# Where the low part of the first weight piece is computed, and a new order for the opening of a fused attention and feed-forward kernel

## The chip, the cores and the metric

The kernel runs on one core of one Trainium2 chip. The metric is the device time of one execution in microseconds (us). TensorE is called PE in the rows, its weight loads PEld, VectorE DVE, ScalarE ACT, GpSimd POOL, SyncE SP; a "q" behind a name is that engine's instruction queue, DMA issues included.

## The reference

A linear attention with a decaying state runs over 768 steps for 4 x 8 heads of 48 channels, and its output goes through a feed-forward layer without biases:

```python
for t in range(S):                                   # B=4, H=8, S=768, D=48
    cur = np.einsum('bhd,bhe->bhde', u[None] * kt, vt)
    y[:, :, t] = np.einsum('bhd,bhde->bhe', rt, state + cur)
    state = wt[:, :, :, None] * state + np.einsum('bhd,bhe->bhde', kt, vt)
x = y.transpose(0, 2, 1, 3).reshape(B * S, H * D)    # 3072 x 384
h = x @ w_in                                         # 384 x 2048
g = h * (1.0 / (1.0 + np.exp(-1.702 * h)))
out = g @ w_out                                      # 2048 x 384
```

All inputs and the output are float32.

## The kernel before

**Tiling.** The 3072 tokens are 24 chunks of 128 tokens, in 6 groups of 4 chunks. Attention works by chunk: VectorE scans the decays (L421, L427) and scales keys and queries (L442, L443), PE forms their products (L450, L476, L507, L525), ScalarE builds diagonal masks (L496), VectorE masks the scores (L576), and PE sums the output of the chunk into `ps_y` (L570, L615, L619). The feed-forward layer works by task: a task is one group (512 tokens) and one block of 128 of the 2048 hidden channels. Its first product (L679) is followed by the gelu (L690 or L694 on ScalarE, L695 on VectorE) and the second product (L709 to L711, later in the row-tiled form of L735).

**Split operands.** A float32 operand is held as two fp32r tiles, a rounded high part and the low part that is left, and each product is made of three: high by high, high by low, low by high. The output of a chunk is split by L633 (ScalarE writes the high part), L637 (PE adds minus the identity times the high part to the same PSUM bank) and L638 (ScalarE copies what is left there). Chunk 3, the last of the first group, is the last that is split before the first task can run, and `fill_x` (L647, token x2) then has twelve issues on SP and POOL move parts of x of chunks 0 to 2 to other partitions; the first task's first three matmuls read the three blocks of x that are so filled.

**Weights.** They arrive in 1 MB pieces (`raw`). `convert(i)`, the tokens "w i", unpacks one: ScalarE L224 and L225, VectorE L227 and L230, ScalarE L233 writes the high part into `pair`, VectorE L235 subtracts it and so writes the low part. Piece 0 is the first that a task needs, pieces 2 and 1 follow.

**Order.** Instructions are issued on each engine in the order of emission. For the opening (the first 20 tasks of 96, and chunks 0 to 10) that order is the hand-written string `RAMP`, whose tokens `do` carries out one by one (L859): "l 4" is a load of chunk 4, "a 3" the next step of chunk 3, "g 0", "h 0" and "y 0" are first product, gelu and second product of task 0, and "k 3" stands for three filler matmuls (`keep_clock`, L724) on a constant tile, whose result nothing uses. A planner orders what comes after `RAMP`. `ps_h` is a pool of two PSUM buffers (tag "ph") that the first products take in turn.

Of the kernel before, what the change touches and what calls it, by code (L numbers as in the profile page):

```python
# [8 lines left out]
F32 = mybir.dt.float32  # L9
# [5 lines left out]
ALU = mybir.AluOpType  # L15
# [6 lines left out]
P = 128  # L22
# [11 lines left out]
NL = SL // 2  # L34
# [26 lines left out]

FIRST = 20
RAMP = """
l0 M l0 a0 a0 a0 l0 k13 a0 a0 l1 l1 l2 a0 a0 a1 k4 a0 a1 f2 a1 l1 a0 l3 a0 k1 a1 a1 a1 a1 a2 f2 k3 a0 a0 w2 a1 a1 a2
f0 a2 k1 a0 a1 a1 l2 a2 a2 a2 k3 a1 a2 l3 a3 f0 a1 a2 a2 a2 w0 a3 f1 a3 a1 k2 a3 a2 f4 a3 w0 a3 k3 a2 a3 a3 a3 l4 a2
w0 a3 a3 a2 a4 f6 w0 a3 w2 x2 a3 w1 w1 k5 a3 k3 g0 f6 w2 g1 l4 w2 a4 h0 g2 f4 a4 w1 w1 h1 g3 w4 h2 w4 f3 a4 a4 a4 f8
y0 w3 f5 l5 g4 w3 h3 m4 l6 w4 a4 y1 w4 a4 w3 a4 g5 a5 w3 y2 a4 h4 a5 l5 a5 h5 y3 g6 w5 w5 m5 y4 a4 a5 w6 w6 h6 f7 w5
w5 w6 a5 w6 a6 g7 f8 w8 a5 y5 l6 w8 h7 g8 g9 w7 y6 a6 a6 a4 w7 a5 y7 w8 w8 a6 f10 h8 f9 u a5 a6 h9 w7 a6 a5 g10 w9
l7 f10 g11 a5 w7 a6 w9 l8 m6 a5 l7 a7 h10 y8 y9 w9 a6 w10 a7 g12 f11 w9 a6 y10 a7 h11 h12 a5 l9 w11 a7 w10 w11 a7 m7
a7 w10 a7 w11 y11 w10 y12 w11 a6 a7 g13 a7 a8 l8 h13 l9 g14 a6 a8 a8 g15 l10 a8 y13 h14 a7 m8 a7 a8 a8 h15 a9 a9 y14  # L70
a8 x7 y15 a8 a9 l10 a8 g16 g17 h16 m9 a9 h17 a9 a9 l11 g18 a9 y16 a10 a8 h18 y17 a9 g19 a10 a10 a8 a10 a9 a10 h19
m10 a10 l11
"""
WIDE = 512
CROSS = 6
HALF = 6
GAP = 3
ALONE = (HALF, 8)
THIRDS = [(m, (2 * m + i) * TOP // D, (2 * m + i) * TOP % D, i == 0) for m in range(NM) for i in range(2)]
WP = NF * DM // NL  # L80
SPLIT = range(FIRST, len(TASKS) - 1)
# [7 lines left out]
def rwkv_ffn_kernel(ctx: ExitStack, tc, wkr, vp, vrk, ub, w_in, w_out, masks, vt, uc, out):  # L89
    nc = tc.nc  # L90
    V, A, G, T = nc.vector, nc.scalar, nc.gpsimd, nc.tensor
# [5 lines left out]
    ps_h = ctx.enter_context(tc.tile_pool(name="ps_h", bufs=2, space=PSUM))  # L97
# [16 lines left out]
    ident = cp.tile([P, P], F32, name="ident")  # L114
# [12 lines left out]
    minus = wt.tile([P, P], F32R, tag=f"w{2 * NL - 2}", name="minus")  # L127
# [88 lines left out]
    def convert(i, pool, clamp):  # L216

        st = staged.pop(i)
        c = pool.tile([P, WP], I32, tag="c", name="c", bufs=2)
        w = st.rearrange("p k (n two) -> p (k n) two", two=2)  # L220
        l, h = w[:, :, 0], w[:, :, 1]
        cf = c.bitcast(F32)
        sums = {} if clamp else dict(accum_out=acc_sum[:, i : i + 1])
        A.activation(l, l.bitcast(U32), AF.Copy, scale=L_SCALE)  # L224
        A.activation(cf, h.bitcast(F32), AF.Abs, scale=W_SHIFT, **sums)  # L225
        yield
        V.scalar_tensor_tensor(h, h, -(2 ** 31), l, op0=ALU.bitwise_and, op1=ALU.bitwise_or)  # L227
        if clamp:
            V.tensor_scalar(cf, cf, W_MAX, None, op0=ALU.min)
        V.scalar_tensor_tensor(c, c, 3, h, op0=ALU.logical_shift_left, op1=ALU.bitwise_or)  # L230
        yield
        pair = pairs[i] = wt.tile([P, 2, WP], F32R, tag=f"w{i}", name=f"pair{i}")
        A.copy(pair[:, 0], cf)  # L233
        yield
        V.tensor_tensor(pair[:, 1], cf, pair[:, 0].bitcast(F32), op=ALU.subtract)  # L235
        yield

    def weight(which, f, m):

# [47 lines left out]
    def one_run(here, ahead):  # L287

        def emit(lists, before=None):

            mm = None
            for x in lists:
                if x:
                    out, w, moving, start, stop = x.pop(0)
                    mm = T.matmul(out, w, moving, start=start, stop=stop, skip_group_check=True)  # L295
                    if before:
                        tc.add_manual_dep(mm.ins, before, SYNC, reason="the other row tile is done with these rows")
                        before = None
            return mm

        same, other = ([ahead[r_][r_ ^ n] for r_ in range(2)] if ahead else [[], []] for n in range(2))
        before = None
        for beside in (other, same) if here else ():
            rows = here.pop(0)
            while max(map(len, rows)):
                mm = emit(rows, before)
                emit(beside)
                before = None
            if beside is other:
                for _ in range(GAP):  # L310
                    emit(same)
                nop = T.nop()
                tc.add_manual_dep(nop.ins, mm.ins.name, SYNC, reason="the rows of the bank change row tiles")
                before = nop.ins.name
        while max(map(len, same + other)):
            emit(same + other)

    def token_halves(t, kf, qf, kt, v, s, sf):
# [17 lines left out]
        for p in range(NP):  # L336
            for h in range(2):
                for b in range(2):
                    ahead[h][b].append(
                        (scores[h][half[b], p], kf[head(h), p, half[b]], qf[head(h), p, half[b]], True, True)  # L340
                    )
        if t in ALONE:
            one_run([], ahead)
# [64 lines left out]
    def chunk(t):  # L408
# [128 lines left out]
        def straight(ps, pair, low, high, rhs):  # L537

            for m in range(NM):
                for h in range(2):  # L540
                    yield ps[h * HB : (h + 1) * HB, m], pair(m, h), rhs(m, h)
            for m, h, d0, up in THIRDS:
                out_, w_ = (ps[P - 2 * TOP :, m], high) if up else (ps[0:TOP, m], low)
# [287 lines left out]
    def count(oks):  # L831

        ps = ps_a.tile([1, 1], F32, tag="psa", name="ps_n")
        T.matmul(ps, oks, oks, start=True, stop=True)
        V.tensor_copy(cnt, ps)
# [5 lines left out]
    with tc.manual_schedule():  # L841
# [7 lines left out]
        running, told = {}, {}  # L849

        def piece(kind, i):

            if (kind, i) not in running:
                running[kind, i] = {
                    "l": load, "e": decays, "a": chunk, "m": measures.get, "w": lambda i: convert(i, su, False), "r": rows_of, "f": fetch
                }[kind](i)
            next(running[kind, i])

        def do(token):  # L859
            kind, i = token[0], int(token[1:] or 0)  # L860
            told[token] = told.get(token, 0) + 1
            if kind in "lamwrfe":
                piece(kind, i)
                if kind == "w" and all(told.get(f"w{n}") == 4 for n in range(2 * NL)):
                    early.close()
                    pools["late"] = fast.enter_context(tc.tile_pool(name="late", bufs=2))
            elif kind == "x":
                group, col = where[i]
                if col == CHUNKS[group] - 1 - (group == 0):
                    fill_x(xs[group], 0, (col + 1) * C)  # L870
            elif kind == "u":
                nc.sync.dma_start(u_sb, ub)
                for x, fill, compare in ((eye, 0.0, ALU.not_equal), (later, 1.0, ALU.is_gt)):
                    G.memset(x, fill)
                    for h in range(2):
                        G.affine_select(
                            out=x[h * HB : (h + 1) * HB], in_=x[h * HB : (h + 1) * HB], pattern=[[1, HB]], base=0,
                            channel_multiplier=-1, compare_op=compare, fill=1.0 - fill,
                        )
            elif kind == "M":  # L880
                A.dma_start(hm[TOP:R2], masks)
                G.dma_start(um[TOP:R2, 0 : H // 2], masks[:, 2 : 2 + H // 2])
                for h in range(2):
                    rows, others = (slice(g * D, (g + 1) * D) for g in (h, 1 - h))
                    G.dma_start(um[TOP:R2][rows, H // 2 :], masks[others, 2 + H // 2 :])
                for x in states + [v[:, 0:TOP] for v in values] + padded:
                    G.memset(x, 0.0)
                A.activation(minus, ident, AF.Copy, scale=-1.0)
            elif kind == "k":
                for _ in range(i):  # L890
                    keep_clock()
            elif kind == "g":
                if i == len(TASKS) - 1:
                    count(counted.pop())
                first_product(i, TASKS[i])
            elif kind == "h":
                gelu(i, TASKS[i])
            elif kind == "y":
                second_product(i, TASKS[i])
            if kind == "y" or kind == "r" and told[token] == 2:  # L900
                i -= LAG if kind == "r" else 0
                parts.pop(i, None)
                group = TASKS[i][0]
                if i == last[group]:
                    if group == len(CHUNKS) - 1:
                        counted.append(nc.values_load(cnt, min_val=0, max_val=full))
                    store(group, starts[group] * C, CHUNKS[group] * C, (1, 0, 2) if kind == "r" else range(NM))
# [44 lines left out]
        for token in RAMP.split():  # L952
            do(token)
# [11 lines left out]
    n = counted[0]  # L965
# [104 lines left out]
```

## Time and profile before

| | us |
|---|---|
| median of 3 runs (lowest, highest) | 485.99 (485.84, 487.25) |
| the profiled execution | 485.96 |
| its span, first to last instruction | 484.2 |
| PE busy in the span | 475.0 (98%) |
| VectorE busy in the span | 289.6 (60%) |
| ScalarE busy in the span | 256.7 (53%) |

The profiled execution lies 0.03 us under the median, and 1.76 us of it lie outside the span. The shares of the whole span hide that it has stages: VectorE's 60% are an average over an opening in which it hardly rests and a later part in which it has little to do.

### The profile page before, as it was taken

To read this page: it belongs to the slowest core of one execution; us is meant where nothing else is said; L and a number is where in the kernel's file an instruction comes from. 1 tells how busy PE (TensorE), PEld (TensorE's weight loads), DVE (VectorE), ACT (ScalarE), POOL (GpSimd) and SP (SyncE) were. 2 spreads that over 40 slices of the span, in tenths; PEclk is the share of its full clock that TensorE was granted. 3 is DMA by queue.
4 is the path that set the end of the run, shared out by engine and by line. 5 is a ranking of instruction groups with operands and counts; after the bars stand their busy time and mean duration, and the time that the engine had idled before them with its cause. 6 is when DMAs were issued, how large, how long until landed. Compare 5 with 4: busy or idle time off the path is not lost.

```text
span 484.2 us, 14345 instructions
## 1 busy us (share of the span) xinstructions
PE 475.0 (98%) x5915; PEld 406.1 (84%) x5915; DVE 289.6 (60%) x455; ACT 256.7 (53%) x611; POOL 106.6 (22%) x222
## 2 busy tenths in 40 slices
PE   7999999999999999999999999999999999999995
PEld 4768888888888888888888888888888888888884
DVE  8999999998776456546656566666574221112120
ACT  5988898875653534634545545545645422422222
POOL 4051000002132406434407235406200002100000
PEclk9999999999999999999999999999999999999998
DMA  8868955235532305224305134205120001100002
GB/s 313 289 251 322 306 166 151 50 100 128 157 86 80 100 3 132 92 74 115 95 8 149 69 101 115 81 20 132 46 89 2 3 1 34 66 2 1 1 0 72
DMA packets 20728, 48.47 MB, mean 100 GB/s; under 512 B 4816, under 2 KB 10032, under 8 KB 20656
## 3 DMA queue, kind: packets, MB, share of 16 engines
q1 hardware_dynamic: 12128, 26.72, 16.6%
q0 software_dynamic: 8128, 20.24, 15.0%
q8 instruction: 48, 0.79, 0.7%
q10 hardware_dynamic: 400, 0.53, 0.3%
q14 instruction: 24, 0.20, 0.1%
HBM read 40.49 MB, written 4.72 MB: 93 GB/s over the span
## 4 chain that ended last, share of the span: by engine, by line
PE 95%; DVE 1%; DMA 1%; issue 1%; ACT 0%; SPq 0%; ACTq 0%; PEldq 0%; DVEq 0%
PE po L735 32%; PE ph L735 30%; PE ph L679 9%; PE ps_c L295 5%; PE ps_a L295 3%; PE po L709 3%; PE po L711 3%; PE po L710 3%; PE ps_d L450 1%; PE ps_y L619 1%; PE ps_t L476 1%; PE ps_y L532 1%; PE ps_s L525 1%; PE ps_t L470 1%; PE idle L724 1%; DMA wkr_t<-in_wkr 1%
## 5 line engine op out<-in xcount | busy, mean ns | idle before, releaser
L735 PE MATMUL ph<-x,pair 64*128 64x512 f32 x1350 | 220.6, 377 | 0.0
L735 PE MATMUL po<-gh,pair 64*128 64x512 f32 x912 | 185.9, 383 | 0.2 <-SPq L740 0.2
L735 PEld LDWEIGHTS ph<-x,pair 64*128 64x128 f32 x1350 | 170.2, 186 | 17.8 <-ACT gf L694 0.6
L695 DVE TENSOR_TENSOR gl<-gf,gh 128x512 fp32r<-128x512 f32 x96 | 66.1, 690 | 146.7 <-ACT gf L694 146.7
L694 ACT ACTIVATE gh<-ph 128x512 fp32r<-128x512 f32 x84 | 49.9, 594 | 150.7 <-PE ph L735 143.5
L735 PEld LDWEIGHTS po<-gh,pair 64*128 64x128 f32 x912 | 113.7, 186 | 12.4 <-issue 0.6
L735 PE MATMUL po<-gl,pair 64*128 64x512 f32 x456 | 117.1, 376 | 0.0
L735 PEld LDWEIGHTS po<-gl,pair 64*128 64x128 f32 x456 | 58.8, 186 | 5.7
L647 POOL DMA_DIRECT2D x<-x x33 | 16.6, 511 | 169.2 <-DVE x L248 127.1
L694 ACT ACTIVATE gf<-ph 128x512 f32<-128x512 f32 x84 | 49.6, 590 | 0.0
L679 PE MATMUL ph<-x,pair 128*128 128x512 f32 x189 | 45.4, 390 | 0.4 <-DMA x<-x 0.3
L679 PEld LDWEIGHTS ph<-x,pair 128*128 128x128 f32 x189 | 35.0, 188 | 7.6 <-DMA x<-x 0.9
L351 ACT ACTIVATE am<-eye,s 128x64 f32<-128x64 f32 x144 | 36.2, 336 | 4.1 <-PE ps_c L295 3.6
L184 POOL DMA_DIRECT2D wkr_t<-in_wkr x72 | 36.1, 505 | 4.8 <-issue 3.2
L248 DVE TENSOR_TENSOR x<-ps_c,x 112x512 fp32r<-112x512 f32 (+1 forms) x20 | 12.6, 638 | 29.5 <-ACT x L247 29.5
L421 DVE TENSOR_TENSOR_SCAN lp<-wkr_t,d1r 112x516 f32<-112x516 f32 x24 | 29.3, 1222 | 1.2 <-DMA wkr_t<-in_wkr 1.0
L427 DVE TENSOR_TENSOR_SCAN lp<-wkr_t,d1f 112x516 f32<-112x516 f32 x24 | 29.4, 1225 | 0.1
L247 ACT ACTIVATE x<-ps_c 112x512 fp32r<-112x512 f32 (+1 forms) x20 | 11.1, 555 | 29.7 <-PE ps_c L295 29.7
L295 PE MATMUL ps_a<-kq 48*64 48x64 f32 (+1 forms) x576 | 26.4, 221 | 0.0
L709 PE MATMUL po<-gh,pair 128*128 128x512 f32 x60 | 23.7, 396 | 0.0
L181 POOL DMA_DIRECT2D wkr_t<-in_wkr x36 | 18.8, 522 | 19.8 <-DVE lp L427 12.1
L711 PE MATMUL po<-gl,pair 128*128 128x512 f32 x60 | 23.2, 386 | 0.0
(128 smaller groups left out, 653.3 us busy)
## 6 DMA issues: line engine op xcount, KB each, us to landing
raw<-in_w_out SPq DMA_DIRECT2D x6, 1024.0 KB, 6.6
raw<-in_w_in SPq DMA_DIRECT2D x5, 1024.0 KB, 8.6
rk_t<-in_vrk POOLq DMA_DIRECT2D x12, 384.0 KB, 4.2
wkr_t<-in_wkr SPq DMA_DIRECT2D x4, 770.5 KB, 8.4
out_t<-ob POOLq DMA_DIRECT2D x12, 256.0 KB, 2.6
v_t<-in_vrk SPq DMA_DIRECT2D x12, 192.0 KB, 3.4
wkr_t<-in_wkr POOLq DMA_DIRECT2D x24, 96.0 KB, 2.5
wkr_t<-in_wkr POOLq DMA_DIRECT2D x48, 48.0 KB, 2.1
```

What stands on the lines that cost most here:

```text
L181: behind_moves(queue[0].dma_start(a[TOP:R2, one], wkr[t, :, one]))
L184: queue[0].dma_start(a[rows, two], wkr[t, (1 - h) * D : (2 - h) * D, two])
L295: mm = T.matmul(out, w, moving, start=start, stop=stop, skip_group_check=True)
L351: A.activation(am[h][:, p], eye, AF.Copy, scale=s[:, j : j + 1])
L421: V.tensor_tensor_scan(li.rearrange("r p c -> r (p c)")[:, ::-1], w1[:, ::-1], d1r.rearrange("r p c -> r (p c)")[:, ::-1], 0.0, op0=ALU.mu ...
L427: V.tensor_tensor_scan(pm.rearrange("r p c -> r (p c)"), w0, d1f.rearrange("r p c -> r (p c)"), 0.0, op0=ALU.mult, op1=ALU.add,)
L679: T.matmul(o, pair[w_], halves(x[:, x_, c, cs], plain), start=k_ == 0, stop=k_ == 3 * NM - 1)
L694: A.activation(g, ph, AF.Gelu_apprx_sigmoid, scale=1.0 / W_SCALE)
L695: V.tensor_tensor(gl, gf, gh.bitcast(F32), op=ALU.subtract)
L709: T.matmul(o, h_, halves(gh, plain), start=first, stop=False, skip_group_check=True)
L711: T.matmul(o, h_, halves(gl, plain), start=False, stop=f == NF - 1, skip_group_check=True)
L735: mm = T.matmul(by_twos(out), w[rows], halves(x[rows]), start=start, stop=stop, skip_group_check=True)
```

## The change

Three things change. For weight piece 0 alone (`RESTS`), the low part is no longer a VectorE subtraction. In two halves of 512 columns, PE multiplies the identity by the unpacked weights (float32 operands) into a `ps_h` buffer, adds minus the identity times the high part (fp32r operands), and ScalarE copies the rest into the low half of `pair`. The step count of piece 0 becomes five. And `RAMP` is written anew, with 303 tokens in place of 298, and 29 fillers in place of 38; the first line of each stands in the diff, their rows below tell more.

```diff
-l0 M l0 a0 a0 a0 l0 k13 a0 a0 l1 l1 l2 a0 a0 a1 k4 a0 a1 f2 a1 l1 a0 l3 a0 k1 a1 a1 a1 a1 a2 f2 k3 a0 a0 w2 a1 a1 a2
+k1 k5 M k2 l0 a0 k4 k2 l0 a0 a0 l1 a1 l1 a0 a1 a0 a0 l1 f2 a0 l0 k3 k1 a0 l2 a1 a0 a0 a1 a1 a1 l3 a1 a2 a0 f2 a1 a1
...
+RESTS = (0,)
...
-        V.tensor_tensor(pair[:, 1], cf, pair[:, 0].bitcast(F32), op=ALU.subtract)
-        yield
+        if clamp or i not in RESTS:
+            V.tensor_tensor(pair[:, 1], cf, pair[:, 0].bitcast(F32), op=ALU.subtract)
+            yield
+            return
+        for q in range(WP // WIDE):
+            cols = slice(q * WIDE, (q + 1) * WIDE)
+            rest = ps_h.tile([P, WIDE], F32, tag="ph", name="rest")
+            T.matmul(rest, ident, cf[:, cols], start=True, stop=False, skip_group_check=True)
+            T.matmul(rest, minus, pair[:, 0, cols], start=False, stop=True, skip_group_check=True)
+            A.copy(pair[:, 1, cols], rest)
+            yield
...
-                if kind == "w" and all(told.get(f"w{n}") == 4 for n in range(2 * NL)):
+                if kind == "w" and all(told.get(f"w{n}") == 4 + (n in RESTS) for n in range(2 * NL)):
```

In the changed kernel a line up to 235 of the old stands one line further down, the subtraction at L237, the new lines at L239 to L246, and the rest ten lines further down.

**TensorE, between the output of chunk 3 and the first task.** Before, from the last product of chunk 3's output (L615) to the first products of tasks 0 to 3 (L679; `pair_472` is weight piece 0, `pair_551` piece 2):

```order
L615 MATMUL ps_y<-am,v_t 16x128
L724 LDWEIGHTS d1r
L724 MATMUL idle<-d1r 128x512
...
L637 MATMUL ps_y<-x,minus 128x384
L724 LDWEIGHTS d1r
L724 MATMUL idle<-d1r 128x512
...
L679 MATMUL ph<-x,pair_472 128x512 x24
L679 MATMUL ph<-x,pair_551 128x512 x12
L450 MATMUL ps_d<-hm,rku 128x2 x4
```

The same place in the changed kernel (`pair_510` is piece 0, `pair_540` piece 2, `rest` the new PSUM tile):

```order
L625 MATMUL ps_y<-am,v_t 16x128
L243 MATMUL rest<-c,ident 128x512
L244 MATMUL rest<-pair_510,minus 128x512
...
L734 LDWEIGHTS d1r
L734 MATMUL idle<-d1r 128x512
L647 MATMUL ps_y<-x,minus 128x384
L689 MATMUL ph<-x,pair_510 128x512 x18
L460 MATMUL ps_d<-hm,rku 128x2 x4
L486 MATMUL ps_t<-ident,kq 128x112 x4
L689 MATMUL ph<-x,pair_510 128x512 x6
L689 MATMUL ph<-x,pair_540 128x512 x12
```

Five fillers ahead of chunk 3's L637 and three behind it (of each run one stands above) have become four products for the rest and one filler, and chunk 4's L450 and L476, which stood behind the first products of tasks 0 to 3, now stand behind those of tasks 0 and 1. Between chunk 0's output (L619) and the first task there were 17 fillers and are 11; just ahead of that output, where four stood, none is left; ahead of chunk 2's L637, behind that same output, stood 9 and stand 10.

**VectorE, from chunk 3's masks on.** Before, L576 masks the last scores of chunk 3, L421 to L443 prepare chunk 4, and the three pieces of weights lie between (`raw_213` is piece 2, `raw_400` piece 1):

```order
L576 COPY_PREDICATED am<-after,ps_s_461 128x512
L421 SCALAR_TENSOR_TENSOR lp<-wkr_t,d1r 112x516
L425 RECIPROCAL d1f<-lp 112x4
L235 TENSOR_TENSOR pair_472<-c,pair_472 128x1024
L227 SCALAR_TENSOR_TENSOR raw_213<-raw_213 128x1024
L230 SCALAR_TENSOR_TENSOR c<-c,raw_213 128x1024
L227 SCALAR_TENSOR_TENSOR raw_400<-raw_400 128x1024
L230 SCALAR_TENSOR_TENSOR c<-c,raw_400 128x1024
L235 TENSOR_TENSOR pair_551<-c,pair_551 128x1024
L427 SCALAR_TENSOR_TENSOR lp<-wkr_t,d1f 112x516
```

In the changed kernel (`raw_189` is piece 2, `raw_468` piece 1):

```order
L586 COPY_PREDICATED am<-after,ps_s_459 128x512
L228 SCALAR_TENSOR_TENSOR raw_189<-raw_189 128x1024
L231 SCALAR_TENSOR_TENSOR c<-c,raw_189 128x1024
L431 SCALAR_TENSOR_TENSOR lp<-wkr_t,d1r 112x516
L435 RECIPROCAL d1f<-lp 112x4
L437 SCALAR_TENSOR_TENSOR lp<-wkr_t,d1f 112x516
...
L453 SCALAR_TENSOR_TENSOR kq<-wkr_t,live,lp 112x512
L228 SCALAR_TENSOR_TENSOR raw_468<-raw_468 128x1024
L231 SCALAR_TENSOR_TENSOR c<-c,raw_468 128x1024
L237 TENSOR_TENSOR pair_540<-c,pair_540 128x1024
```

The subtraction of piece 0 is gone, piece 2's unpacking stands first, all of chunk 4's preparation comes ahead of piece 1, and the subtraction of piece 2 stays behind the unpacking of piece 1.

**ScalarE, from the split of chunk 3 on.** Before, L633 of chunk 3 (three blocks of 128) was followed by the unpacking of piece 1:

```order
L633 ACTIVATE x,acc<-ps_y 128x3x128
L224 ACTIVATE raw_400<-raw_400 128x1024
L225 ACTIVATE c,acc<-raw_400 128x1024
L638 CAST x<-ps_y 128x3x128
L233 CAST pair_551<-c 128x1024
```

In the changed kernel, with the two copies of the rest behind it:

```order
L643 ACTIVATE x,acc<-ps_y 128x3x128
L245 CAST pair_510<-rest 128x512 x2
L648 CAST x<-ps_y 128x3x128
L234 CAST pair_540<-c 128x1024
L225 ACTIVATE raw_468<-raw_468 128x1024
L226 ACTIVATE c,acc<-raw_468 128x1024
```

The unpacking of piece 1 has moved behind the copies of the rest, the split of chunk 3 and the high part of piece 2.

Behind these places, the last 3435 rows of TensorE and all rows of GpSimd stand in the same order as before. On SyncE's queue the values of chunk 0 move from third place to seventh, behind the first 1 MB of weights.

## Rows read from the trace of the kernel before

**Rows 1.** Windows: us, busy (x) of PE PEld DVE ACT POOL, PEclk, DMA, GB/s

```profile
11.00:13.60 2.60, 2.46 (x18) 1.63 (x16) 2.60 (x5) 1.28 (x6) 0.00 (x0) 1.00 1.05 417
13.60:34.50 20.90, 20.89 (x271) 16.08 (x270) 20.66 (x32) 18.63 (x49) 5.88 (x13) 1.00 0.81 280
```

**Rows 2.** Waits of PE, whole span: waiting line, releaser, idle us, count, longest

```profile
PE idle L724 <- POOL d1r L108: 2.4, 1, 2.4
...
PE ph L679 <- DMA x<-x: 0.3, 1, 0.3
```

**Rows 3.** Chain that ended last, 20 to 36 us: start, us, engine, line

```profile
28.01 1.09 PE ps_s L525 x16
...
32.55 2.59 DMA x<-x
...
35.79 0.47 PE ph L679
```

**Rows 4.** The same chain, whole span, the first tasks

```profile
35.79 7.99 PE ph L679 x34
```

**Rows 5.** Timeline of TensorE, 2 to 45 us: start, us, what; in brackets idle before

```profile
2.39 4.91 PE L724 MATMUL idle<-d1r 112*128 112x512 bf16 x13 [2.39 <-POOL d1r L108]
...
13.61 1.40 PE L619 MATMUL ps_y<-am,v_t 128*64 128x128 f32 x15
...
23.73 0.49 PE L637 MATMUL ps_y<-x,minus 112*112 112x512 f32 x1
...
24.06 0.61 PE L724 MATMUL idle<-d1r 112*128 112x512 bf16 x2
...
30.61 0.49 PE L637 MATMUL ps_y<-x,minus 112*112 112x512 f32 x1
31.02 0.64 PEld L615 LDWEIGHTS ps_y<-am,spare 128*64 128x64 f32 x12 [0.25 <-issue]
...
32.08 0.27 PE L615 MATMUL ps_y<-am,spare 128*32 128x128 f32 x1
...
32.19 0.27 PE L615 MATMUL ps_y<-am,spare 128*32 128x128 f32 x1
...
32.61 1.25 PE L724 MATMUL idle<-d1r 112*128 112x512 bf16 x5
33.51 0.52 PE L637 MATMUL ps_y<-x,minus 128*128 128x384 f32 x1
34.49 0.47 PE L679 MATMUL ph<-x,pair 128*128 128x512 f32 x1
...
43.62 0.95 PE L450 MATMUL ps_d<-hm,rku 112*128 112x2 f32 x8
...
44.77 0.47 PE L709 MATMUL po<-gh,pair 128*128 128x512 f32 x1
```

**Rows 6.** Timeline of VectorE and ScalarE, 31 to 48 us, columns as in rows 5

```profile
31.81 1.20 DVE L235 TENSOR_TENSOR pair<-c,pair 128x1024 fp32r<-128x1024 f32 x1
...
33.21 1.17 ACT L224 ACTIVATE raw<-raw 128x1024 int32<-128x1024 uint32 x1
34.26 1.15 ACT L225 ACTIVATE c<-raw 128x1024 f32<-128x1024 f32 x1
...
35.39 0.48 ACT L638 CAST x<-ps_y 128x384 fp32r<-128x384 f32 x1
35.54 1.23 DVE L227 SCALAR_TENSOR_TENSOR raw<-raw 128x1024 int32<-128x1024 int32 x1
35.75 1.07 ACT L233 CAST pair<-c 128x1024 fp32r<-128x1024 f32 x1
...
37.94 1.26 DVE L235 TENSOR_TENSOR pair<-c,pair 128x1024 fp32r<-128x1024 f32 x1
...
43.85 1.28 DVE L695 TENSOR_TENSOR gl<-gf,gh 128x512 fp32r<-128x512 f32 x2
...
47.44 0.35 DVE L461 TENSOR_TENSOR sf<-sf,lp 112x192 f32<-112x192 f32 x1
```

More of the change, by code (lines that the diff above doesn't have):

```diff
@@ L63 @@
 RAMP = """
-l0 M l0 a0 a0 a0 l0 k13 a0 a0 l1 l1 l2 a0 a0 a1 k4 a0 a1 f2 a1 l1 a0 l3 a0 k1 a1 a1 a1 a1 a2 f2 k3 a0 a0 w2 a1 a1 a2
[L65 to L72, printed above, removed]
+k1 k5 M k2 l0 a0 k4 k2 l0 a0 a0 l1 a1 l1 a0 a1 a0 a0 l1 f2 a0 l0 k3 k1 a0 l2 a1 a0 a0 a1 a1 a1 l3 a1 a2 a0 f2 a1 a1
+a0 k1 a2 k1 a2 w2 k5 a2 a2 a1 a0 f0 a1 a2 a3 l2 a1 f0 k1 l3 k1 a2 a3 k1 a2 l4 a2 a2 a1 a2 a3 a3 w0 a3 a1 w0 a3 f4 a2
+l4 a3 a3 a3 f1 a3 f4 a3 a2 a2 w2 a3 w0 a3 w0 w0 a4 a4 x2 f3 l5 k1 a3 w2 g0 w1 g1 f6 a4 a4 f11 w1 w2 h0 f6 l6 h1 w1
+w4 a4 w1 w4 a4 l5 w3 f5 f8 g2 w3 g3 h2 y0 w4 w4 h3 m4 y1 w3 g4 w3 a5 h4 a5 l6 w6 g5 y2 f9 w5 w6 w5 h5 f8 a4 g6 a4 f7
+w6 a4 y3 w6 a4 g7 y4 w5 w5 a5 w8 a5 h6 a4 a5 m5 a4 w8 h7 w7 a6 g8 u a6 a5 y5 a5 w8 y6 a6 a5 h8 y7 g9 w8 w7 g10 a5 m6
+w9 l7 l8 a5 h9 a6 a6 w9 a6 g11 f10 f10 h10 l7 a6 a5 w7 w9 w7 a7 w10 w9 y8 a7 h11 a6 a6 w10 y9 g12 w11 a7 y10 a5 w11
+a7 a7 w10 w10 a7 a7 h12 l9 y11 a6 w11 w11 m7 g13 a6 a8 g14 h13 l8 a8 a7 a8 g15 a7 a8 y12 h14 y13 a8 h15 m8 a7 a9 l9
+a7 a9 a8 y14 l10 x7 a9 y15 l10 a8 m9 a8 a9 a8 a9 a9 g16 h16 g17 a10 a10 a9 h17 g18 a8 y16 a10 a9 g19 a9 h18 l11 a8
+l11 a10 h19 a10 y17 a10 m10
 """
```

## The prediction

> **What bounds the kernel now.** I read the waits of TensorE (PE) first, then the chain that ended last, then the windows and the timeline of the opening. From its first filler on, PE hardly waits: the longest idle time in the list is that before the first filler, 2.4 us, and what bears on this change is 0.3 us in the first product (L679), ended by the DMA that moves x [rows 2]. The chain says the same: up to 35.79 us it runs through that move (2.59 us) and into the first product's third matmul, and then 34 matmuls follow in 7.99 us, 0.235 each, with no gap [rows 3, 4]. From chunk 0's output at 13.61 to the first task at 34.49 PE is busy in 20.89 of 20.90 us, but part of that is fillers [rows 1, 5]. VectorE is nearly as full there, 20.66 of 20.90 us [rows 1]: by its busy share alone it could be the bound of the opening. It isn't the one that PE is seen to wait for. VectorE's subtraction for weight piece 0 (L235) ran from 31.81 to 33.01, and the moved x arrived only at 32.55 + 2.59 = 35.14 [rows 3, 6].
>
> Since behind the first task PE has no wait that could absorb anything, I take the end to shift as much as the first task does, plus whatever new stalls come behind it.
>
> **What the change takes from PE.** A filler costs (1.25 − 0.61) / 3 = 0.213 us (five took 1.25, two 0.61) [rows 5]. Between chunk 0's output and the first task six are gone: −1.28. The four that stood ahead of that output lie outside this stretch; there VectorE was busy in 2.60 of 2.60 us [rows 1], and sets when the output starts, so I cost their loss at nothing (what it may do to the clock is a rival).
>
> **What it adds to PE.** Each half of the rest is a float32 product of 512 columns and an fp32r product of 512. The trace has no float32 product of this size. L615, with 128 columns, starts one pass 0.11 us after the other (32.08, 32.19) [rows 5], and a float32 product has two passes here (eight L525 products of 128 columns in the program are the 16 records of rows 3). So 4 x 2 x 0.11 = 0.88. Bounds: by L525, which covers 1024 columns in 1.09 us [rows 3], 512 cost 0.545; if L525 owes that to two products that run side by side on halves of the rows, a product over all rows pays 1.09. I take 0.88, which is the spacing of two passes over the same rows. The fp32r product costs 0.235 among its like, but when a float32 product follows, the next starts 0.42 later (30.61 to 31.03, with 0.25 idle before the weight load), and when a filler follows 0.33 (23.73 to 24.06) [rows 5]. The rest is thus 0.88 + 0.42 + 0.88 + 0.33 = 2.51, at the lower end 2 x (0.545 + 0.235) = 1.56, at the upper 2 x 1.09 + 0.42 + 0.33 = 2.93.
>
> Here a rule speaks against the 0.42. The Trainium skill, "TensorE: Matmul & The Clock Gate", section "Step-by-step: what each phase is for", says that PE pulls weight loads ahead of matmuls in flight. By it the load would be hidden and the rest would cost an estimated 2 x (0.88 + 0.235) = 2.23, and the whole sum below would be some 486.5. The row at L615 shows the load after 0.25 us idle, so here the trace does not agree.
>
> **When the first task starts.** PE arrives at 34.49 − 1.28 + 2.51 = 35.72 (ends 34.77 and 36.14). Its third matmul, two places on, could start at 35.72 + 0.47 = 36.19. Before, it started at 35.79, held by the move. The move follows chunk 2's L637, ahead of which (behind chunk 0's output) stand ten fillers instead of nine; so it comes 0.21 later and allows the third matmul at 36.00. PE is the later: 36.19, **+0.40** (ends +0.21, where the move decides, and 36.61, +0.82). The low part of piece 0 itself hides: ScalarE's copies of 512 columns run beside the filler and chunk 3's L637, and the low part is first read by the fourth matmul.
>
> **What is late next.** VectorE loses one L235, 1.20 us [rows 6]. But piece 2's subtraction stands behind piece 1's unpacking on VectorE, and that waits for ScalarE, where the two copies, chunk 3's L638 and piece 2's high part now stand ahead of piece 1. Followed step by step: chunk 3's L637 starts some 0.35 ahead of the first task, at 35.37, and lasts 0.52 [rows 5]; L638 starts at 35.89; piece 2's high part 0.36 later (35.39 to 35.75), 36.25; L224 1.07 later, 37.32; L225 1.05 later (33.21 to 34.26), 38.37; VectorE's L227 1.28 later (34.26 to 35.54), 39.65; the subtraction of piece 2 2.40 later (35.54 to 37.94), 42.05; it ends 1.26 later, 43.31 [rows 6]. PE first reads that low part in the ninth matmul of the third task (g2). From the third matmul of the first task it has 16 to the end of the second, 16 x 0.235 = 3.76, then chunk 4's L450 and L476, 1.15 (43.62 to 44.77, where they stand in a row) [rows 5], and eight more, 1.88: it arrives at 36.19 + 6.79 = 42.98. **A stall of 0.33.** Queued behind it on PE are the fourth task and the first second products, nothing else can run. Next VectorE makes two L695 (1.28), one L461 (0.35) and piece 1's subtraction (1.20) [rows 6], up to 43.31 + 2.83 = 46.14, while PE, with ten matmuls and the first of y0, 11 x 0.235, reads that low part at 45.89: at most 0.25 more, and 0 if the L695 overlap as they may; I take **0.1**.
>
> Together 0.40 + 0.33 + 0.10 = +0.83 on the profiled execution: 485.96 + 0.83 = **486.8**.
>
> What else moves I cost at nothing. Chunk 0's values, behind 1 MB of weights in SyncE's queue, are read some way into chunk 0, behind the scans of VectorE, and VectorE had no pause there. The rest shares `ph` with the first products, both buffers of which are free at that point. The conversion of piece 0's high part has the 12 products of L615 to hide behind.
>
> **The rivals.** A change within 0.3% (1.46 us) can't be told from none by a measurement of this kernel; so "faster" begins under 484.5 and "slower" over 487.45.
>
> 1. As summed: 486.8, its own range 486.2 to 487.4 (arrival at either end). Chance 0.52.
> 2. It does next to nothing: PE arrives ahead of the move (rest at its lower end), and piece 2 is ready in time because ScalarE gets to it sooner. Only the move's 0.21 is left: 486.2. For it speaks that L525 covers columns at the lower price. Chance 0.16.
> 3. Faster: VectorE was the bound. Its 20.66 busy of 20.90 us speaks for it; that PE never waits for VectorE in the list, and that the move arrives 2.1 us after the subtraction ends, against. If the 1.20 counts in full, 485.96 − 1.20 = 484.75; if the new order also brings the move forward, so that the first three matmuls (34.49 to 35.79, where 0.47 would do [rows 5]) lose 0.5 less, 484.25. It decides if the third matmul starts before 35.3. Chance 0.16, some 0.10 of it under the bound.
> 4. Slower: the float32 product costs its upper bound, which puts PE, chunk 3's split and all behind it 0.42 later (487.2), and VectorE, which idles some 1.8 us up to 39.65 for ScalarE and saves only 1.20, carries the 0.6 into the next tasks: 487.8. Chance 0.10.
> 5. Slower through the clock. At the start, 13 fillers took 4.91 us where 13 x 0.213 is 2.77 [rows 5]: many ran at the lower of the two levels, 1.2 GHz, which doubles a filler, though the clock column reads 1.00 where shown. With the four fillers ahead of chunk 0's output gone, PE's busy time from 11.0 to 13.6 falls from 2.46 to about 1.6 us [rows 1]. If the clock falls there and has to come up again, I price that as at the start, 4.91 − 2.77 = 2.1: 488.9. Against it: 1.6 of 2.6 us is still work, and products surround it. Chance 0.06.
>
> The Trainium skill, "TensorE: Matmul & The Clock Gate", section "What's actually happening", says that the throttled state is the default and that activity lifts it; the slow first fillers agree, and no run here shows yet how it falls.
>
> **How the numbers follow.** The time is that of rival 1. Under 484.5 lies 0.10 (of 3), over 487.45 some 0.06 of 4, the 0.06 of 5 and 0.01 of 1's tail: 0.13; the other 0.77 is no change that can be told. The range from 484.6 to 488.0 leaves out the faster part of 3, the clock and the tail of 4, just under 0.2.
>
> **What would show it.** In the profile after: L243 at 0.88 us each (0.55 or 1.09 would be the bounds); the load before the second identity product after 0.25 idle; the third matmul of the first product at about 36.2, released by nothing or by L245, not by the DMA; PE's idle 0.3 us before a first product at about 43, ended by VectorE's L237; L228 of piece 1 at about 39.6 after VectorE's longest pause in the opening. Fillers 0.43 apart after 11 us, or a clock below 1.00 there, would show the fifth. The sum is wrong if chunk 0's output does not start at 13.6: everything behind it hangs on that row, and an order that brings it forward gives back all of it.

## The result, and the profile after

The changed kernel took 493.63 us (median of 5, 488.80 to 496.22) against 486.13 (median of 5 for the kernel before). The ratio is 1.0128, 95% interval 1.0103 to 1.0153: slower by 6.2 us by the ratio and 7.5 by the medians, well outside the 484.6 to 488.0 that were forecast. The ratio leaves out the slowest execution, which lies over 1.5% above the fastest. The five executions lie unusually far apart, and their mean granted clock goes with it: 0.999 in the fastest, 0.986 to 0.992 in the other four. The profiled one is the slowest, 496.22, with a span of 494.5; what its trace shows is therefore set beside the traces of the variants below.

The waits of TensorE (PE) in the changed kernel, which answer to [rows 2] (waiting line, releaser, idle us, count, longest):

```profile
PE idle L734 <- POOL d1r L109: 2.4, 1, 2.4
PE ps_u L517 <- DMA v_t<-in_vrk: 2.3, 1, 2.3
PE ph L689 <- DMA x<-x: 1.9, 1, 1.9
PE ps_t L486 <- DVE kq L452: 1.7, 1, 1.7
```

The first line is unchanged. The other three are new, 5.9 us together. Two of them lie outside all that the prediction looked at. The chain that ended last, up to 45 us:

```profile
3.63 8.15 DMA v_t<-in_vrk
...
11.92 0.64 PE ps_u L517 x13
...
40.12 4.24 PE ph L689 x18
```

PE waits for the values of chunk 0 (`v_t`), issued at 3.63 behind 1 MB of weights and landed 8.15 later. Chunk 0's output starts at 16.50 instead of 13.61, and the first task at 39.95 by the timeline (40.12 is the chain's, which counts from the end of the instruction before), where 35.72 was forecast. The wait alone does not make up these 4.2 us; the windows show the rest (columns as in [rows 1]; the third number from the end is the granted clock):

```profile
9.00:12.00 3.00, 0.70 (x6) 0.21 (x5) 2.93 (x5) 2.67 (x9) 0.00 (x0) 1.00 1.04 421
12.00:13.40 1.40, 1.40 (x30) 1.35 (x32) 0.83 (x2) 0.32 (x1) 0.00 (x0) 0.94 1.01 423
13.40:20.00 6.60, 6.60 (x56) 6.01 (x56) 3.56 (x7) 3.50 (x12) 0.00 (x0) 0.50 0.93 244
```

PE is busy in 0.70 of 3.00 us, and afterwards the granted clock reads 0.50, the 1.2 GHz level, for 6.6 us. PE looks full there, but in 6.60 us it makes 56 records; in the same stretch of e7 below, at a clock of 1.00, it makes 85. VectorE, which waits for PE, is busy in 3.56 of them.

The other two waits come much later. Pieces of the same chain, 84 to 132 us:

```profile
86.23 5.05 DMA raw<-in_w_in
91.31 4.12 DMA raw<-in_w_in
...
95.50 1.14 ACT raw L225
...
126.12 4.95 DMA x<-x
```

Weight piece 10 is loaded only at 86.23, because its tokens (f10) stand behind those that load chunks 7 and 8, which wait on SyncE's queue for buffers. ScalarE stands until it lands (95.50), and all that follows on VectorE is late, up to `kq` (the 1.7 us). The 1.9 us are the moved x of the second group, ahead of task 16. In the traces of e1 and e9 below, which load piece 10 in the same late place, ScalarE waits 1.40 and 0.99 us for it (3.09 here) and PE does not wait for `kq` at all: that wait belongs to this execution, not to the place of the load alone.

### The profile page after: what moved, and what is told of

Its sections match the earlier page's. It is cut to its first block, busy times and chain, and to the rows that moved or that the text cites. A ratio compares the mean times of both kernels' runs of the same rounds, so it can differ in the third digit from the quotient of the medians.

```text
span 494.5 us, 14337 instructions
## 1 busy us (share of the span) xinstructions
PE 480.0 (97%) x5912; PEld 410.1 (83%) x5912; DVE 289.0 (58%) x454; ACT 258.0 (52%) x613; POOL 104.5 (21%) x222
## 4 chain that ended last, share of the span: by engine, by line
PE 79%; DMA 8%; DVE 6%; ACT 2%; SPq 2%; issue 2%; POOL 0%; ACTq 0%; PEldq 0%; DVEq 0%; POOLq 0%
PE po L745 31%; PE ph L745 30%; PE ps_c L305 5%; DMA raw<-in_w_in 4%; PE ps_a L305 3%; PE ph L689 3%; DMA v_t<-in_vrk 2%; DVE raw L228 1%; DMA x<-x 1%; DVE pair L237 1%; PE ps_d L460 1%; SPq L185 1%; PE ps_y L629 1%; PE ps_e L535 1%; DVE c L231 1%
## 5 line engine op out<-in xcount | busy, mean ns | idle before, releaser
L185 POOL DMA_DIRECT2D wkr_t<-in_wkr x72 | 36.0, 505 | 6.2 <-issue 3.2
L431 DVE TENSOR_TENSOR_SCAN lp<-wkr_t,d1r 112x516 f32<-112x516 f32 x24 | 29.4, 1223 | 2.0 <-DMA wkr_t<-in_wkr 1.1
L258 DVE TENSOR_TENSOR x<-ps_c,x 112x512 fp32r<-112x512 f32 (+1 forms) x20 | 12.6, 636 | 27.3 <-ACT x L257 27.3
L719 PE MATMUL po<-gh,pair 128*128 128x512 f32 x60 | 24.1, 401 | 0.0
L720 PE MATMUL po<-gh,pair 128*128 128x512 f32 x60 | 23.7, 394 | 0.0
```

The costliest lines, as they stand in the source:

```text
L185: queue[0].dma_start(a[rows, two], wkr[t, (1 - h) * D : (2 - h) * D, two])
L431: V.tensor_tensor_scan(li.rearrange("r p c -> r (p c)")[:, ::-1], w1[:, ::-1], d1r.rearrange("r p c -> r (p c)")[:, ::-1], 0.0, op0=ALU.mu ...
L719: T.matmul(o, h_, halves(gh, plain), start=first, stop=False, skip_group_check=True)
L720: T.matmul(o, l_, halves(gh, plain), start=False, stop=False, skip_group_check=True)
```

## The experiments

The kernels of one set ran on the same chip. Numbers are medians, with the lowest and highest; "before" is the kernel before on that chip. The changed kernel itself was measured apart from them (486.13 for the kernel before there).

| run | us | before | ratio, 95% interval |
|---|---|---|---|
| e1 values early | 489.62 (488.62 to 493.34) | 486.33 | 1.0069 [1.0041, 1.0097] |
| e2 piece 10 early | 492.36 (489.37 to 495.97) | 486.33 | 1.0100 [1.0068, 1.0132] |
| e3 both | 488.99 (488.54 to 491.61) | 486.33 | 1.0059 [1.0033, 1.0085] |
| e6 before, values late | 491.66 (487.94 to 493.27) | 486.33 | 1.0088 [1.0054, 1.0123] |
| e4 before, products | 487.65 (487.30 to 494.54) | 486.42 | 1.0022 [1.0013, 1.0031] |
| e7 e3, task 13 behind | 487.29 (487.01 to 487.49) | 486.42 | 1.0014 [1.0006, 1.0023] |
| e8 e7, subtracting | 488.34 (486.70 to 490.00) | 486.42 | 1.0034 [1.0021, 1.0046] |
| e9 changed, filled | 493.19 (489.74 to 495.01) | 486.42 | 1.0148 [1.0128, 1.0167] |
| e10 e7, values late | 491.61 (488.10 to 493.81) | 486.29 | 1.0110 [1.0072, 1.0149] |
| e11 e10, filled | 489.06 (487.93 to 489.76) | 486.29 | 1.0051 [1.0033, 1.0068] |
| e12 e8, filled | 487.77 (487.20 to 488.41) | 486.29 | 1.0030 [1.0018, 1.0042] |
| e13 e4, split first | 488.38 (487.70 to 489.29, and once 1298.34) | 486.29 | 1.0036 [1.0024, 1.0048] |
| e14 e7, piece 2 first | 486.96 (486.55 to 488.09) | 486.15 | 1.0006 [0.9975, 1.0036] |
| e15 three fillers fewer | 486.97 (486.45 to 499.75) | 486.15 | 1.0011 [0.9986, 1.0037] |
| e16 seven fewer | 487.11 (486.34 to 488.69) | 486.15 | 1.0010 [0.9987, 1.0033] |

**First set: which of the waits cost the time?** The theories were A, the late values; B, the late piece 10; C, the products for the rest.

e1 moves one token, the load of chunk 0's values, to the front:

```diff
-k4 k2 l0 a0 a0 l1 a1 l1 a0 a1 a0 a0 l1 f2 a0 l0 k3
+k4 k2 l0 l0 a0 a0 l1 a1 l1 a0 a1 a0 a0 l1 f2 a0 k3
```

> The changed kernel with one token moved: the load of chunk 0's values goes back to third place in SyncE's queue, ahead of the 1 MB of weights. Theory A (the values land at 11.79, PE idles 2.30 us for them, and the granted clock then falls to 0.50 from 13.4 to 20): the wait and the fall both go, chunk 0's output starts near 13.6 again instead of 16.50, and the first task near 35.7 instead of 40.12; the time falls by 2.9 to 5.2 us from 493.6, to 488.4 to 490.7, and what is left over the kernel before is the later stalls. Theory B (the later stalls around 97 to 131 us, behind the late load of weight piece 10, are the loss and the opening's delay is absorbed): 492 to 495. Theory C (the products for the rest are the loss): 493, no change.

e2 moves the loads of piece 10, and e3 makes both moves:

```diff
-w9 l7 l8 a5 h9 a6 a6 w9 a6 g11 f10 f10 h10
+w9 f10 f10 l7 l8 a5 h9 a6 a6 w9 a6 g11 h10
```

> The changed kernel with the two loads of weight piece 10 moved ahead of the loads of chunks 7 and 8 in SyncE's queue, chunk 0's values still late. Theory A: the opening's wait and clock fall stay, the stalls of 1.72 us at L486 and 1.9 us for the moved x go: 493.6 - 3.6 = 490.0, not below 489. Theory B: 487 to 488.5, since the opening does not count. Theory C: 493.

> Both moves of the two runs above in one kernel. Theory A with the later stalls as an independent second loss: 493.6 - 5.2 - 3.6 = 484.8 to 487, about the time of the kernel before. Theory B: as with piece 10 alone. Theory C (the products for the rest cost it): still 490 or more.

e6 is the kernel before with the loads of the opening in the changed kernel's order:

```diff
-a0 a0 a0 l0 k13 a0 a0 l1 l1 l2 a0 a0 a1 k4 a0 a1 f2 a1 l1 a0 l3
+a0 a0 a0 k13 a0 a0 l1 l1 a0 a0 a1 l1 f2 l0 l2 k4 a0 a1 a1 a0 l3
```

> The kernel before with the loads of the opening in the changed kernel's order in SyncE's queue (chunk 0's values seventh, behind 1 MB of weights), nothing else changed. Theory A: PE waits about 2 us for the values around 10 us, and in most executions the clock falls behind it: 488.5 to 491.5. If the lateness is hidden, or absorbed by the fillers that follow (17 of 0.213, 3.6 us), 486 to 487.

One token gives back 4.0 us by the medians (493.63 to 489.62; 2.9 by the ratios), and the same lateness put into the kernel before costs it 5.3 (4.3 by the ratio; its 491.66 lies 0.16 over the range expected for it): A holds in both directions. In e6 the wait and the clock fall are there too (its waits, then its windows):

```profile
PE ps_u L507 <- DMA v_t<-in_vrk: 1.7, 1, 1.7
```

```profile
9.00:12.00 3.00, 1.31 (x13) 0.61 (x12) 2.93 (x5) 2.77 (x9) 0.00 (x0) 0.85 1.04 423
13.40:20.00 6.60, 6.60 (x40) 5.14 (x40) 2.98 (x5) 2.37 (x9) 0.00 (x0) 0.50 0.86 230
```

B missed, and so did A's own sum for the later waits: piece 10 alone gave 1.3 us where 3.6 were expected, on top of the values 0.6, and e3 stayed 2.7 over the kernel before, which fits none of the three. In both comparisons the intervals overlap (e2 and the changed kernel, e3 and e1), and the longest wait behind the opening is the same 1.5 us in the traces of e1 and e3: what the place of piece 10 costs is not shown. In e2 the later wait had not gone but grown, to 2.8 us for the moved x. The chain of e3 shows the same place:

```profile
119.03 4.38 DMA x<-x
123.41 0.14 issue
123.54 4.77 PE ph L689 x21
```

The move that brings the second group's x into place for task 16 ran until 123.41, and PE waited 1.5 us for it. Two things made it late. Chunk 7's output starts 0.9 us later on PE than in the kernel before (112.90 and 112.00), and on VectorE a scan (L431) now stands ahead of the last step of the split (L258, L248 before), which has to wait 0.6 us for it. The kernel before, then e3:

```profile
114.13 0.79 DVE L248 TENSOR_TENSOR x<-ps_c,x 112x256 fp32r<-112x256 f32 x2 [1.75 <-ACT x L247]
```

```profile
114.14 1.22 DVE L431 TENSOR_TENSOR_SCAN lp<-wkr_t,d1r 112x516 f32<-112x516 f32 x1
...
115.50 0.73 DVE L258 TENSOR_TENSOR x<-ps_c,x 112x256 fp32r<-112x256 f32 x2
```

So the six transfers of the move are issued 1.3 us later; and the last of them takes twice as long. The view of the tile `x` around there, of the kernel before and of e3:

```profile
L647 POOL DMA_DIRECT2D x<-x x6: 504/507/522, 115.2 to 117.7; - x6
...
DMA to landing us min/median/max: 2.2/2.4/2.6
```

```profile
L657 POOL DMA_DIRECT2D x<-x x6: 507/507/522, 116.5 to 119.0; - x6
...
DMA to landing us min/median/max: 2.1/2.7/4.4
```

In e3 SyncE issues the stores of an output block (L824) from 118.27 on, ahead of the last transfer of the move; in the kernel before they come from 118.66 on, behind it. That these stores slow it is the likely reading; no run tests it alone.

**Second set: the rest of the loss, the products, and the clock.** In both kernels the second product of task 13 (y13) stands ahead of chunk 7's output. e7 puts it behind, so that the output comes earlier and more work hides the move, and the scan behind the split:

```diff
-y12 h14 y13 a8 h15 m8 a7 a9 l9 a7 a9 a8 y14
+y12 h14 a8 h15 m8 a7 l9 a7 y13 a9 a9 a8 y14
```

> The third kernel of the first set (values and piece 10 early) with the second product of task 13 moved behind chunk 7's output, and the scan of chunk 9 behind the end of chunk 7's split. Theory A: the 1.5 us that PE waits at the first product of task 16 for the moved x go, 489.0 - 1.5 = 487.5 (486.9 to 487.8), and 0.5 to 1.0 stay over the kernel before, the opening's. Rival: the wait moves to another place of the opening (the new order of VectorE), 488.5 to 489.5.

It hit: 487.29, with the executions within 0.5 us and the move's wait gone: its transfers are issued from 115.2 to 117.7 again, and none takes longer than 2.5 us. Which of the two changes did it, the runs do not tell apart. e8 is e7 with the subtraction back on VectorE (`RESTS = ()`, and one w0 fewer):

> The kernel above with the low part of piece 0 subtracted on VectorE again (no products, no copies, fillers as they are). Theory A: PE reaches the first task 2.5 earlier, but the moved x holds the third matmul at about 36, and piece 2's low part comes up to 1.2 later: within 0.5 of the kernel above. Theory C (the products cost what they take): 2 us or more less than the kernel above, 485 to 485.5. Theory D (VectorE bounds the opening): 1.2 more, 488.7.

It took 488.34, which fits none of the three cleanly: its best executions, 486.70 and 486.75, are faster than e7, ten of twelve slower or equal, nine with a mean clock of 0.990 to 0.994. Its windows tell why:

```profile
34.00:36.00 2.00, 1.23 (x12) 0.47 (x6) 2.00 (x3) 1.38 (x4) 1.89 (x5) 1.00 0.36 82
36.00:38.00 2.00, 1.34 (x3) 0.80 (x4) 1.93 (x3) 2.00 (x3) 1.82 (x4) 0.86 0.23 65
38.00:40.00 2.00, 2.00 (x6) 1.52 (x6) 2.00 (x4) 1.24 (x3) 1.26 (x2) 0.50 0.56 147
```

Without the products PE idles in 1.4 of 4 us ahead of the moved x, and then the clock is at 0.50 as the first task runs.

e4 is the kernel before with the products alone, in place of its last eight fillers:

```diff
-w0 a3 a3 a2 a4 f6 w0 a3 w2 x2 a3 w1 w1 k5 a3 k3 g0
+w0 a3 a3 a2 a4 f6 a3 w2 x2 a3 w0 w0 w1 w1 a3 g0
```

> The kernel before with only the low part of piece 0 changed: the four products and two copies stand where its last eight fillers stood (five ahead of chunk 3's L637, three behind), the VectorE subtraction is gone, the loads and the rest of the order are as before. Theory A (the loads' order is the loss, the products themselves hide): PE reaches the first task at 34.49 - 8 x 0.213 + 2.5 = 35.3, the moved x still lets the third matmul start at 35.8, 485.5 to 486.9, no change. Theory C (products on PE cost what they take, fillers are free): 486.3 + 2.5 = 488.8. Theory D (VectorE's 1.20 was the bound): 485.1.

487.65, 1.2 over before, between A and C. The waits name a cause, though in a profiled execution unlike the others (494.54; the last section comes back to it):

```profile
PE ph L689 <- ACT x L648: 1.3, 1, 1.3
```

The last step of the split of chunk 3 stood behind the copies of the rest and the unpacking of piece 1 on ScalarE. A further kernel (e13) set that right and missed too:

```diff
-x2 a3 w0 w0 w1 w1 a3 g0
+x2 a3 w0 w0 a3 w1 w1 g0
```

> The kernel before with the products (487.65, with 1.3 us of waiting for chunk 3's L648, which stood behind the unpacking of piece 1 on ScalarE), now with that L648 ahead of the unpacking. Theory A (the products hide, the wait was my placement): 487.65 - 1.3 = 486.4, the time of the kernel before; piece 2's low part may come later and take up to 0.5 back. Theory C (products cost): 487.5 or more.

It took 488.38, more than e4's 487.65. L648's wait was gone, and in its place PE waited 0.9 us in two pieces for gelus (L700) that the unpacking now held up, and 0.7 us for values. This only moved the wait. It looks as if ScalarE had no room for the two copies in the old order; no run tests that.

e9 is the changed kernel with eleven more fillers (the expectations of e9 and e11 count twelve) where PE waits for the values (`k3 k1` becomes `k3 k12`):

> The changed kernel, its loads untouched, with twelve more fillers (2.6 us) ahead of the product that waits for chunk 0's values, so that PE is busy while it waits. If the idle time is what lets the clock fall: the granted clock stays at 1.00 from 12 to 21, the values' 2.3 us of delay stay, and the time falls from 493.6 to about 489.5 to 491, with few executions above. If the clock falls for another reason (the transfers, or the opening as a whole): 493 to 496.

It was inconclusive: in the profiled execution the clock stayed at 1.00 from 9 to 24 us and the time was 489.74, but the other three took 493 to 495 with a mean clock of 0.991 to 0.994. The kernel still waits for the moved x later on (1.4 us in that execution), and no trace tells which wait let the clock fall.

**Third set: lateness and clock without the late waits.** e10 is e7 with e1's move undone; e11 adds e9's fillers to it.

> The kernel with values, piece 10 and task 13 set right (487.3), and of these only the values of chunk 0 late again, as in the changed kernel. This prices the values' lateness by itself. Theory A (wait of about 2.3, then the clock falls in most executions and costs up to 3.4 more): 489.6 to 492.5, spread over 3 us. If the lateness cost only its wait: 489.6, close together. If it were absorbed: 487.3.

> The kernel above with twelve more fillers in place of the idle time ahead of the product that waits for the values. If PE's idle time is what lets the clock fall: the wait's 2.3 us stay, the clock does not fall, 489.3 to 490.2 and close together. If the fall comes from the transfers or from anything else in the opening: as the kernel above, spread over 3 us.

e10 took 491.61: the late values alone cost 4.3 us. Two of its six executions, 488.10 and 488.26, kept a mean clock of 0.999, the other four have 0.987 to 0.990 and 491.6 to 493.8. With PE kept busy, e11's six all have 0.997 to 0.999 and none is above 489.76. The windows of the profiled executions, first e10 (one that kept its clock), then e11:

```profile
9.00:12.00 3.00, 1.51 (x15) 0.81 (x15) 2.93 (x5) 2.62 (x9) 0.00 (x0) 1.00 1.02 411
```

```profile
9.00:12.00 3.00, 3.00 (x19) 1.69 (x19) 2.93 (x5) 2.45 (x9) 0.00 (x0) 1.00 1.02 417
```

So the 4.3 us are about 0.9 of delay (488.2 against 487.29) and, in two executions of three, 3.4 to 5.6 of clock; and it is PE's idle time that lets the clock fall, for the loads stand in the same order in both. Six executions of each carry this, and none of e10 with a fallen clock was profiled; the fall itself is in the traces of the changed kernel and of e6. e10's profile puts the 1.5 us ahead of L517 down to a ScalarE mask (L506), which that product does not read; its `v_t`, issued at 3.63, landed 8.1 us later, at 11.7, and it starts at 11.87. The fillers have a price too: e11's median lies 0.9 over the two executions of e10 that kept their clock.

The Trainium skill, "TensorE: Matmul & The Clock Gate", section "What's actually happening", has the throttled state as the default that activity lifts; e10 and e11 agree.

e12 asks the same of e8: eleven more fillers stand where the products stood (`k1 a3 w2 g0` becomes `k12 a3 w2 g0`).

> The kernel in which the low part of piece 0 is subtracted on VectorE (488.3, mean clock 0.993 in most executions), with eleven more fillers (2.3 us) where the products for the rest stood. If the products mattered only as work that keeps PE busy up to the moved x: the clock stays up and it takes 486.7 to 487.5, as the kernel with products. If VectorE's 1.2 us count: 488.0 or more although the clock stays. If the clock falls for another reason than PE's idle time there: 488.3 as before.

487.77, between the first two ranges, and all eight with a clock of 0.996 to 0.998. So it was PE's idle time there that let e8's clock fall. In time the fillers won little (0.6 us by the medians, 0.2 by the ratios, whose intervals overlap): the two executions of e8 at 486.70 and 486.75, which kept their clock without them, lie under all of e12. Over e7 stay 0.5 us by the medians, 0.8 by the ratios, and these intervals overlap as well; in e12's trace PE waits 0.5 for L444 on VectorE. If the products are worth anything in place of fillers, it is less than the 1.2 us of the subtraction.

**Fourth set: what is left in the opening.** e14 puts piece 2's subtraction ahead of piece 1's unpacking (`w1 w2 h0` becomes `w2 w1 h0`); e15 takes three of the seven fillers ahead of chunk 2's L460 away (`w2 k5` becomes `w2 k2`), e16 four more (three ahead of chunk 2's L517, one ahead of g0).

> The kernel with values, piece 10 and task 13 set right (487.3), with piece 2's subtraction on VectorE ahead of piece 1's unpacking. In its trace PE waits 0.20 for that subtraction at 43.4. If this wait is part of the 0.9 that stay over the kernel before: 486.9 to 487.1. If it only moves the wait to piece 1: 487.3.

> The kernel above with three of the seven fillers between chunk 1's scores and chunk 2's L460 left out (0.64). If PE, with its fillers and products, is what sets the start of the first task at 35.80: 486.3 to 486.5. If VectorE sets it (its chain of scans and masks): no change, 486.9 to 487.3, with a wait of PE for VectorE in their place; if PE's idle time lets the clock fall, 488 or more.

> The kernel above with the next three fillers (ahead of chunk 2's L517) and the one ahead of the first task left out too (0.85 more). If PE sets the start: 485.5 to 485.7, under the kernel before. If VectorE or the moved x sets it: as the kernel above, or the clock falls in some executions, 487 to 489.

In e14's trace the wait for piece 2 is gone, but its median lies 0.81 over the kernel before on its chip, where e7's lay 0.87: too little to tell. Its interval holds 1, wide as it is by two executions of the kernel before at 492.6 and 492.7; but none of its twelve is under 486.55, and 21 of the 29 of the kernel before are. e15 won nothing more: in its trace the first task starts at 35.81, as in e14 and e7, and PE waits for VectorE where the fillers were (waits of e15; in e14 the two are 0.3 and 0.5):

```profile
PE ps_d L460 <- DVE rku L444: 0.8, 2, 0.6
PE ps_y L629 <- DVE am L586: 0.5, 1, 0.5
```

In e16 the first task starts at 35.25: 1.49 us of fillers gave 0.55, and the median did not move. Four of its twelve executions have a mean clock of 0.993 to 0.996 (487.31 to 488.69), lower than any of e7's eleven: part of what the fillers cost may have come back as clock. None of the kernels beats the one before.

## Why the prediction was wrong

The number of the sum held, for a kernel that waits only where the prediction looked. e7 has the products, the fillers and, in the opening, the order of VectorE and ScalarE of the changed kernel, and it is 0.87 slower than before on its chip (487.29 against 486.42), where +0.83 was forecast. Its timeline answers to the steps one by one:

```profile
33.11 1.13 PE L243 MATMUL rest<-c,ident 128*128 128x512 f32 x2
33.67 0.79 PE L244 MATMUL rest<-pair,minus 128*128 128x512 f32 x1
34.30 1.02 PE L243 MATMUL rest<-c,ident 128*128 128x512 f32 x2
...
35.40 0.39 PE L734 MATMUL idle<-d1r 112*128 112x512 bf16 x1
...
35.80 4.32 PE L689 MATMUL ph<-x,pair 128*128 128x512 f32 x18
...
43.41 2.57 PE L689 MATMUL ph<-x,pair 128*128 128x512 f32 x10 [0.20 <-DVE pair L237]
```

```profile
39.66 1.23 DVE L228 SCALAR_TENSOR_TENSOR raw<-raw 128x1024 int32<-128x1024 int32 x1 [1.61 <-ACT c L226]
...
42.14 1.22 DVE L237 TENSOR_TENSOR pair<-c,pair 128x1024 fp32r<-128x1024 f32 x1
```

The rest takes 33.11 to 35.40, 2.29 where I had 2.51. By the chain of e7 two passes over 512 columns take 0.86 (0.88 forecast) and the fp32r product behind them 0.23: the term that was too large is the 0.42 with its exposed weight load, which in e7 starts at 34.07 while the product before it runs to 34.46. The Trainium skill's rule of weight loads pulled ahead ("TensorE: Matmul & The Clock Gate", section "Step-by-step: what each phase is for"), which I had set aside for one row, gave an estimated 2.23 and was nearer.

The first task starts at 35.80 (35.72 forecast), VectorE's pause ends at 39.66 (39.65), piece 2's subtraction starts at 42.14 (42.05), PE's stall ends at 43.41 (43.31) and lasts 0.20 (0.33). That these agree to 0.1 us is in part luck: the start of the first task is 0.22 early by the rest, 0.17 late by chunk 0's output (13.78 instead of 13.61), and 0.13 late by what no term names. So is the total: the profiled executions of e7 and of the kernel before lie 1.30 apart (487.26 and 485.96), of which the third matmul's 0.48 (36.27 instead of 35.79) and the stall's 0.20 make up about half.

What failed are two steps around it. First, "What else moves I cost at nothing. Chunk 0's values, behind 1 MB of weights in SyncE's queue, are read some way into chunk 0, behind the scans of VectorE". Nothing was worked out there, and it was the largest loss, about 4 us (4.0 in e1 and 4.3 in e10 by the medians, 2.9 and 4.7 by the ratios). The trace of before held the number. There, too, one transfer of values, chunk 1's, stood right behind the 1 MB of weights. The view of the tile `v_t`, 0 to 14 us, of the kernel before:

```profile
L187 SPq DMA_DIRECT2D v_t<-in_vrk x3: 430/431/489, 1.7 to 13.4; - x3
...
DMA to landing us min/median/max: 3.8/5.8/8.4
```

Chunk 0's, in third place, landed 3.8 us after its issue; chunk 1's, issued at 4.11, took 8.4. An issue at 3.63 had to be expected at about 12, not before PE's use of it at 9.3.

Second, "I take the end to shift as much as the first task does, plus whatever new stalls come behind it". I followed the stalls to the first second products and took the rest of the order, in which a long last stretch of PE's rows agrees, as neutral. But the new string reaches up to task 19, and what e3 and e7 change there is worth 2.3 us (489.62 in e1 to 487.29 in e7). 1.7 of it, from e3 to e7, go with the wait for x at task 16, which comes of a later end of the split and of a last transfer that took 4.4 us instead of 2.6 at most; the 0.6 of piece 10 are not clear of noise.

The rivals: that the change does nothing (2) and that VectorE was the bound (3) did not come. e15 and e16 show that 3 was not far: with a few fillers fewer VectorE is what PE waits for, so the six fillers that went were most of what fillers could give there. The identity products at their upper bound (4) did not come either. The clock (5) fell, and more than the 2.1 us I priced; but not from the missing fillers, which are missing in e7 too, whose clock stays at 0.997 to 1.000. It fell behind a wait that I had not seen. The prediction's last sentence named the row that would decide it, chunk 0's output at 13.6, and 0.06 as the chance of a falling clock was far too little for an opening whose clock hangs on PE never waiting.

## What to carry to other kernels

When an order is written anew, follow every transfer that has changed its place in its queue from issue to landing, by a transfer of the kernel before that stood behind the same neighbour, before any instruction is costed. Follow the new order to its end, at each place where a move or a load is only just hidden, not to the end of the edit, and ask what a move that is issued later will run beside. And where fillers keep the clock, price a wait on TensorE not by its length but with the clock that it may cost: in e10 a wait of 1.5 us cost 0.9 by itself, and 3.4 to 5.6 more in the four executions of six whose clock fell.

## What was not expected of the hardware

The clock's fall is not certain: with PE busy in 1.51 of 3.00 us, e10's profiled execution kept a clock of 1.00, while four of its other five had 0.987 to 0.990 on average. One kernel then spreads over 6 us, and a single execution says little.

The clock column can read 1.00 while PE runs at half its speed. In the profiled execution of e4 (494.54, where its other eleven took 487.3 to 487.9), the timeline and a window show:

```profile
13.09 2.08 PE L535 MATMUL ps_e<-kq 64*128 64x128 f32 x16
```

```profile
14.00:18.00 4.00, 4.00 (x26) 3.65 (x25) 2.67 (x4) 0.17 (x1) 0.00 (x0) 1.00 1.00 237
```

Sixteen records of L535 take 2.08 us there, 1.16 elsewhere, though no wait preceded them: durations tell the level when the column does not. Why the clock did not come up earlier in that execution stays open. The kernel before has such executions too: 3 of 35 in the first set took 492.57 to 493.13 and 2 of 29 in the fourth 492.56 and 492.66, at a mean clock of 0.998 or 0.999. None of them was profiled.
